# First batch of a Fourier-filter and feed-forward kernel: split PSUM evacuations, finer filter and x pieces, small operations on GpSimd, another order of the last units

## The chip, the cores and the metric

The kernel runs on one core of a Trainium2 chip. The metric is device time in microseconds (us) of one execution; the median over several executions counts. The core has four compute engines that the profile calls PE (TensorE, matrix products), DVE (VectorE), ACT (ScalarE) and POOL (GpSimd), and SP (SyncE), which here only issues DMAs. DMAs are issued on two queues: POOL's (software descriptors, q0 in the profile) and SP's (hardware descriptors, q1). Each engine takes its instructions in the order of the program; engines wait for each other by semaphores.

## The reference

Eight sequences of 3008 tokens by 256 channels are filtered in the frequency domain, and each token then goes through a gated feed-forward layer:

```python
X = rfft(x, axis=1)                        # x: 8 x 3008 x 256, float32
Y = X * (filt_r + 1j * filt_i)[None]       # 1505 frequencies x 256
t = irfft(Y, n=3008, axis=1).reshape(24064, 256)
h = t @ w_in                               # 256 x 2048
g = h * (1 / (1 + exp(-beta * h)))         # beta: 2048
out = g @ w_out                            # 2048 x 256, float32
```

## The kernel before

**Arithmetic.** The transform of length 3008 = 47 x 64 is done by matrix products in bfloat16, in four stages: stage 1 (table `t1`, 94 rows in, 96 out) mixes the 47-point index, stage 2 (`t2`, one 128 x 128 table for each of NK = 24 frequency groups) the 64-point index; the result is multiplied by the filter (`fr_sb`, `fi_sb`); stages 3 and 4 (`t3` with its rotated copy `t3s`, and `t4`) go back. The tables are computed on the chip at the start from index patterns (POOL iotas, DVE integer arithmetic, ACT sines). The feed-forward layer takes 512 tokens at a time: two matmuls give 128 hidden units (`hps`, L732), ACT applies the gate (L741), four matmuls accumulate the output (`acc`, L752).

**Two phases.** Batches 1 to 7 are filtered inside the feed-forward loop of the batch before, by a plan of steps (L655 to L718). Batch 0 has no such cover: it is filtered first, by an order written out by hand (L300 to L555), while only loads for later run beside it. The first `hps` matmul ends this first phase. The change touches the first phase alone.

**The first phase.** x of batch 0 is loaded as `x0` (32 columns of 94 rows) by five DMAs on POOL's queue (L182 to L192, 8, 8, 8, 4 and 4 columns). `s1_0(g)` (L247) is stage 1 on four columns for both halves of the channels (e = 0, 1) in a two-bank PSUM tile, and one evacuation to `aT`, on DVE or ACT; the last group is evacuated in halves by both. `spin` runs matmuls on zeros. `t2_half` writes half of `t2` (DVE arithmetic L226, L146; ACT sine L230), `t2_shift` derives the other half on DVE (L240, L242). `t3_part` transposes `t2` into `t3` on PE, `a0_turn` transposes `aT` into `a0`.

Then come six units (`units`, L469): three frequency thirds (kg) for e = 0, then three for e = 1. For each, `s2_0` (L422) has 8 matmuls and two DVE products with `fr_sb` and `fi_sb` (L434); `s3_0` (L437) has 16 matmuls and one evacuation to `zT` on ACT. After the three units of one e, `z_turn` transposes `zT` into `zz0`, and `f_0` or `s4_0` does stage 4 and evacuates to `y`. The last unit's evacuation is split over DVE and ACT, both reading one PSUM tile (`split`, L455), and the last two transposes of e = 1 share a tile in `z_pair` (L488). PSUM tiles come from `bank2` (three two-bank buffers) and `turn8` (two buffers of one bank).

**The filter.** Its values are needed on all 128 partitions. `load_filters` (L84) loads 32 partitions of `fr_sb` from SP and the 32 next to them, in reverse order, from POOL, and likewise for `fi_sb`; `spread(n)` (L462) copies a unit's `fr_sb` to the other 64 partitions and its `fi_sb` from there, with two POOL copies. Both DVE products of a unit wait for these copies. The pieces (`parts`, L93) are the three thirds of e = 0, then one third and two thirds of e = 1. SP holds its filter loads back until a two-element DMA, `seen` (L313), which reads the end of `t2` that `t2_shift` writes. Each queue has eight semaphores for DMAs, so a ninth DMA waits for the first to land.

**POOL's queue**, in the order of the program: x loads between iotas, six filter DMAs for parts 0 to 2, the halving of the first rows of `t4` (L298, after ACT has written `t4`), the two DMAs of part 3, `spread(0)`, two DMAs of part 4, `spread(1)`, `spread(2)`, the load of `w_in` (L502), two memsets, `spread(3)`, x of batch 1 (`load_x`), `spread(4)`, `load_x`, `spread(5)`, two `load_x`, and two scalings of `w_out` (L375).

Of the kernel before, what the change touches and what calls it, by code (L numbers as in the profile page):

```python
# [10 lines left out]
P = 128  # L11
# [11 lines left out]
M = 64  # L23
H = M // 2
NK = 24
# [11 lines left out]
def kernel(  # L37
# [52 lines left out]
            src = AP(filt.tensor, filt.offset + off * D + d0, [[N1 * D, H], [sg * D, n], [1, d1 - d0]])  # L90
            eng.dma_start(dst[q0 : q0 + H, k0:k1, d0:d1], src)

    parts = ((0, KH, 0, E2), (KH, 2 * KH, 0, E2), (2 * KH, NK, 0, E2), (0, KH, E2, D), (KH, NK, E2, D))  # L93

    t1 = consts.tile([NP, KP], BF16, name="t1", tag="t1")
    t4 = consts.tile([KP, NP], BF16, name="t4", tag="t4")
# [14 lines left out]
    def evac(dst, src, on_act, scale=None):  # L111
        if on_act:
            nc.scalar.activation(dst, src, ACT.Copy, scale=1.0 if scale is None else scale)  # L113
        elif scale is None:
            nc.vector.tensor_copy(dst, src)  # L115
        else:
            nc.vector.tensor_scalar_mul(dst, src, scale)  # L117
# [15 lines left out]
    def bank2(shape, dt=F32):  # L133
        return spsum.tile(shape, dt, name="sps", tag="sps")

    def turn8():
        return tpsum.tile([P, KH, P], BF16, name="tps", tag="tps")

    def small(name, dt=F32):
        return sp.tile([P, 1], dt, name=name, tag=name)  # L140
# [38 lines left out]
    def load_x0(j0, j1):  # L179
        load_rows(x0[:, j0:j1, :], 0, j0, j1)  # L180

    load_x0(0, 8)  # L182
    iota(ip[:], [[0, 1]], ch=1)
    iota(kc[:], [[1, NK], [0, 2]])
    iota(cc[:], [[0, NK], [1, 2]], base=1)
    load_x0(8, 16)
    iota(vi[:, :, :H], [[1, NK], [N1, H]])
    load_x0(16, 24)
    iota(vi[:, :, H:], [[1, NK], [-N1, H]], base=N1 * (M - 1))
    load_x0(24, 28)  # L190
    make_identity(nc, ident)
    load_x0(28, 32)  # L192
    for part in parts[:3]:
        load_filters(nc.gpsimd, *part)
    with nc.allow_non_contiguous_dma(reason="2048 values, once"):
        nc.sync.dma_start(beta_sb[:], moe_beta.rearrange("(fb fp) -> fp fb", fp=P))
    def shift_and(name, sh, mask):
        t = small(name, I32)
        if sh:
            nc.vector.tensor_scalar(t[:], ip[:], sh, mask, ALU.logical_shift_right, ALU.bitwise_and)  # L200
        else:
            nc.vector.tensor_scalar(t[:], ip[:], mask, None, ALU.bitwise_and)
        return t

    def affine(name, src, mul, add):
        t = small(name)
        nc.vector.tensor_scalar(t[:], src[:], mul, add, ALU.mult, ALU.add)
        return t

    n1s = affine("n1s", shift_and("n1_i", 1, M - 1), TURN / N1, 0.0)  # L210
# [34 lines left out]
    aTv = aT[:].rearrange("p e k (g m) -> p g e k m", m=MG)  # L245

    def s1_0(g, engines):  # L247
        ps = bank2([P, NDC, 512])
        for e in range(NDC):
            for i in range(MG):  # L250
                nc.tensor.matmul(
                    ps[:, e, i * KP : (i + 1) * KP],
                    lhsT=x0[:NP, g * MG + i, e * P : (e + 1) * P],
                    rhs=t1[:],
                    start=True,
                    stop=True,
                )
        src = ps[:, :, : MG * KP].rearrange("p e (m k) -> p e k m", k=KP)
        if len(engines) == 1:
            evac(aTv[:, g], src, engines[0])  # L260
        else:
            for e in range(NDC):
                evac(aTv[:, g, e], src[:, e], engines[e])

    def spin(n):
        ps = tpsum.tile([P, 512], F32, name="tps", tag="tps")
        for _ in range(n):
            nc.tensor.matmul(ps[:], lhsT=rest[:, :P], rhs=rest[:], start=True, stop=True)

    def a0_turn(kg, e, on_act):  # L270
        tp = turn8()
        for kk_ in range(KH):
            k4 = 4 * (kg * KH + kk_)
            nc.tensor.transpose(
                tp[:, kk_, :], aT[:, e, k4 : k4 + 4, :].rearrange("p c j -> p (c j)"), ident[:]
            )
        evac(a0[:, kg * KH : (kg + 1) * KH, e * P : (e + 1) * P], tp[:], on_act)
# [16 lines left out]
    def turn_t4():  # L294
        tp = turn8()
        nc.tensor.transpose(tp[:KP, 0, :NP], t1[:], ident[:NP, :NP])
        nc.scalar.activation(t4[:], tp[:KP, 0, :NP], ACT.Copy)
        nc.gpsimd.tensor_scalar(t4[0:4], t4[0:4], 0.5, None, ALU.mult)  # L298

    spin(17)  # L300
    t1v = t1[:].rearrange("p (k q) -> p k q", q=2)
    for q in range(2):
        nc.scalar.activation(t1v[:, :, q], sn[:NP], ACT.Copy, scale=q_p[q][:NP])
    t2_half(0)
    t2_half(1)
    s1_0(0, (False,))
    s1_0(1, (True,))
    spin(4)
    t2_shift(0)
    t2_shift(1)  # L310
    nc.vector.memset(t2[:, 0, M : P : M - 1], 0.0)
    seen = sp.tile([1, 2], BF16, name="seen", tag="seen")
    nc.sync.dma_start(seen[:], t2[:1, 1, P - 2 :])  # L313
    for part in parts:
        load_filters(nc.sync, *part)
    nc.scalar.activation(warm[:], ms[:], ACT.Silu)
    s1_0(2, (False,))
    s1_0(3, (True,))
    t3_part(0, True)
    v_i = shift_and("v_i", 5, 1)  # L320
    rot = (affine("rot0", v_i, 2.0, -1.0), affine("rot1", v_i, -2.0, 1.0))
    sgn = affine("sgn", c_i, -2.0, 1.0)
    c10 = sp.tile([P, P], BF16, name="c10", tag="c10")
    for c in range(2):
        nc.vector.tensor_copy(c10[:, c * M : (c + 1) * M], t2[:, 0, (1 - c) * M : (2 - c) * M])
    tiny = sp.tile([P, NFB], F32, name="tiny", tag="tiny")
    nc.vector.tensor_tensor(tiny[:], beta_sb[:], beta_sb[:], ALU.mult)
    nc.vector.tensor_scalar(tiny[:], tiny[:], 1e-12, 2e-6, ALU.is_lt, ALU.mult)
    nc.vector.tensor_tensor(beta_sb[:], tiny[:], beta_sb[:], ALU.add)
    nc.vector.reciprocal(rbeta_sb[:], beta_sb[:])  # L330
    s1_0(4, (False,))
    s1_0(5, (True,))
    t3_part(1, True)
    s1_0(6, (False,))
    turn_t4()
    s1_0(7, (False, True))
    t3_rotate(1, KH, False)
    a0_turn(0, 0, False)
    a0_turn(1, 0, True)
    t3_part(2, True)  # L340
    t3_rotate(KH, 2 * KH, False)

    r_sq.close()

# [45 lines left out]
    zz0 = zz0pool.tile([KP, J, D], BF16, name="zz0", tag="zz0")  # L390
    y_tile(0)

    def z_turn(e, hh, on_act):
        tp = turn8()
        for i in range(KH):
            j0 = (hh * KH + i) * KP
            nc.tensor.transpose(tp[:, i, :], zT[e][:, j0 : j0 + P], ident[:])  # L397
        evac(zz0[:, hh * KH : (hh + 1) * KH, e * P : (e + 1) * P], tp[:KP], on_act)
# [35 lines left out]
            nc.vector.tensor_tensor(r_t[:], ps[:], filt[:, ks, ds], ALU.mult)  # L434
            pq[n, c] = r_t

    def s3_0(n, split=False):  # L437
        kg, e = units[n]
        ps = bank2([P, KH, P])
        for c, tab in enumerate((t3, t3s)):  # L440
            src = pq.pop((n, c))
            for kk_ in range(KH):
                nc.tensor.matmul(  # L443
                    ps[:, kk_, :],
                    lhsT=src[:, kk_, :],
                    rhs=tab[:, kg * KH + kk_, :],
                    start=c == 0 and kk_ % 4 == 0,
                    stop=c == 1,
                    skip_group_check=True,
                )  # L450
        kq = P // J
        dst = zT[e][:, :WZ].rearrange("p (j k) -> p j k", k=KP)
        dst = dst[:, :, kg * KH * kq : (kg + 1) * KH * kq]
        src = ps[:].rearrange("p k (c j) -> p j (k c)", j=J)
        if split:  # L455
            for h in range(2):
                js = slice(h * J // 2, (h + 1) * J // 2)
                evac(dst[:, js], src[:, js], h == 1)
        else:
            evac(dst, src, True)  # L460

    def spread(n):  # L462
        kg, e = units[n]
# [21 lines left out]
            inv_scale,  # L485
        )

    def z_pair(e, hh, engines):  # L488
        tp = spsum.tile([P, 2, KH, P], BF16, name="sps", tag="sps")
        for h in range(2):  # L490
            for i in range(KH):
                j0 = ((hh + h) * KH + i) * KP
                nc.tensor.transpose(tp[:, h, i, :], zT[e][:, j0 : j0 + P], ident[:])
        for h in range(2):
            evac(zz0[:, (hh + h) * KH : (hh + h + 1) * KH, e * P : (e + 1) * P], tp[:KP, h], engines[h])

    load_filters(nc.gpsimd, *parts[3])
    spread(0)
    load_filters(nc.gpsimd, *parts[4])
    spread(1)  # L500
    spread(2)
    nc.gpsimd.dma_start(win_sb[:], moe_w_in.rearrange("(dc p) f -> p dc f", p=P))  # L502
    for e in range(NDC):
        nc.gpsimd.memset(zT[e][:, WZ:], 0.0)
    spread(3)
    load_x(1, 0)
    spread(4)
    load_x(1, 1)
    spread(5)
    load_x(1, 2)  # L510
    load_x(1, 3)
    load_wout(0)
    load_wout(WG)
    scale_wout(0)
    scale_wout(WG)

    s2_0(0)
    tp0 = turn8()
    nc.tensor.transpose(tp0[:, 0, :], c10[:], ident[:])
    nc.scalar.activation(t3s[:, 0, :], tp0[:, 0, :], ACT.Copy, scale=sgn[:])  # L520
    a0_turn(2, 0, True)
    s2_0(1)
    t3_rotate(2 * KH, NK, True)
    s3_0(0)
    s2_0(2)
    a0_turn(0, 1, True)
    s3_0(1)
    s2_0(3)
    a0_turn(1, 1, True)
    s3_0(2)  # L530
    s2_0(4)
    a0_turn(2, 1, True)
    z_turn(0, 0, True)
    z_turn(0, 1, True)
    s3_0(3)
# [2 lines left out]
    f_0(0, 1, True)  # L538
    z_turn(0, 2, True)
    z_turn(0, 3, True)  # L540
    f_0(0, 2, True)
    f_0(0, 3, True)
    s3_0(4)
    f_0(0, 4, True)
    f_0(0, 5, True)
    s3_0(5, True)
    f_0(0, 6, False)
    f_0(0, 7, True)
    z_turn(1, 0, False)
    z_turn(1, 1, True)  # L550
    z_pair(1, 2, (False, True))
    s4_0(1, 0, False)
    s4_0(1, 1, True)
    s4_0(1, 2, False)
# [246 lines left out]
```

## Time and profile before

| what | value |
| --- | --- |
| median of 5 runs | 787.03 us (785.72 to 788.42) |
| the profiled execution's own time | 785.72 us |
| its span | 783.9 us, so 1.8 us lie around the span |
| PE busy, share of the span | 762.8 us, 97% |
| DVE, ACT, POOL busy | 436.4, 561.7, 155.7 us |
| first matmul of the feed-forward loop | 42.95 us after the start of the span |

The page gives busy times, a picture of the span in 40 slices, the costliest groups of instructions and the chain of work that ended last. In a group, the columns are line, engine, operation, output and inputs with their shapes, count, then busy time and mean duration, then idle time before and who ended it. In a timeline, a line has the start, the duration, the engine, the line of the program and the tile, and in brackets the idle time before it. As most of the span is one steady loop bound by PE, the first 43 us have to be read by themselves.

### The profile page before, as it was taken

The page shows a single profiled execution, that of the slowest core. Times are in us where ns is not written, and L with a number is a line of the kernel's source. Part 1 is how long each engine was busy: PE and PEld are TensorE (multiplying, and loading weights), DVE is VectorE, ACT ScalarE, POOL GpSimd, SP SyncE. Part 2 cuts the span into 40 slices and gives each one's busy share as a digit, 9 for nine tenths or more (in the row PEclk, how much of TensorE's full clock was granted, in tenths as well). Part 3 has the DMA queues.
Part 4 walks back from the last instruction along what each step waited for, and adds up shares of the span by engine and source line. Part 5 has one row for each costly group of instructions (what it writes and reads, how often), then busy time and mean ns, then how long its engine had stood idle before and what let it go on. Part 6 is the DMA issues. An engine that isn't in the chain of part 4 may idle for free.

```text
span 783.9 us, 15141 instructions
## 1 busy us (share of the span) xinstructions
PE 762.8 (97%) x5971; PEld 544.1 (69%) x6063; DVE 436.4 (56%) x686; ACT 561.7 (72%) x827; POOL 155.7 (20%) x162
## 2 busy tenths in 40 slices
PE   7799999999999999999999999999999999999997
PEld 4666767766677667866678666786667766676665
DVE  8747754776557665566655675466655666321001
ACT  6887867766676766777667776677766777777776
POOL 7824300322012120122101222012200222000000
PEclk9999999999999999999999999999999999999999
DMA  9958276234831349133580416712164211500101
GB/s 184 229 164 199 93 211 167 68 88 110 234 89 57 96 120 243 51 78 105 116 241 28 123 60 158 198 57 86 49 188 118 65 48 49 155 28 28 55 28 54
DMA packets 87067, 88.50 MB, mean 113 GB/s; under 512 B 5629, under 2 KB 77821, under 8 KB 86997
## 3 DMA queue, kind: packets, MB, share of 16 engines
q1 hardware_dynamic: 82420, 72.37, 31.4%
q0 software_dynamic: 4576, 15.17, 11.2%
q8 instruction: 47, 0.77, 0.4%
q14 instruction: 24, 0.19, 0.1%
HBM read 54.47 MB, written 46.66 MB: 129 GB/s over the span
## 4 chain that ended last, share of the span: by engine, by line
PE 94%; DVE 2%; ACT 1%; issue 1%; DMA 1%; POOL 1%; SPq 0%; POOLq 0%; DVEq 0%; ACTq 0%
PE acc L752 43%; PE hps L732 39%; PE ps L578 3%; PE ps L645 3%; PE ps L623 3%; PE ps L594 2%; DMA fr_sb<-in_filt_r_dram 1%; ACT zz L113 0%; PE sps L443 0%; ACT zT L113 0%; PE tps L397 0%; DVE y L117 0%; DVE u L226 0%; POOL fr_sb L466 0%; DVE u L146 0%
## 5 line engine op out<-in xcount | busy, mean ns | idle before, releaser
L741 ACT ACTIVATE gT<-hps,beta_sb 128x512 bf16<-128x512 f32 x752 | 516.7, 687 | 207.6 <-PE hps L732 187.0
L752 PE MATMUL acc<-wout_sb,gT 128*128 128x256 bf16 x3008 | 453.4, 272 | 2.5
L732 PE MATMUL hps<-y,win_sb 128*128 128x512 bf16 (+7 forms) x1636 | 428.2, 350 | 1.0 <-DVE y L117 0.7
L752 PEld LDWEIGHTS <-gT 128*128 128x128 bf16 x3008 | 287.5, 98 | 126.2 <-issue 1.2
L613 POOL TENSOR_TENSOR yh<-a_t,b_t 128x512 bf16<-128x512 f32 x84 | 106.4, 1266 | 420.4 <-DVE b_t L612 419.5
L732 PEld LDWEIGHTS <-win_sb 128*128 128x128 bf16 x1728 | 164.8, 98 | 25.0 <-issue 1.0
L115 DVE COPY ost<-acc 128x512 f32<-128x512 f32 x93 | 59.9, 685 | 146.9 <-PE acc L752 146.9
L115 DVE CAST a<-ps 96x512 bf16<-96x512 f32 x104 | 70.9, 685 | 51.9 <-PE ps L578 47.9
L608 DVE TENSOR_TENSOR a_t<-ps,fr_sb 128x512 f32<-128x512 f32 x84 | 58.1, 691 | 71.1 <-PE ps L594 70.1
L117 DVE TENSOR_SCALAR y<-ps 128x376 bf16<-128x376 f32 x104 | 55.9, 547 | 59.3 <-PE ps L645 59.1
L609 DVE SCALAR_TENSOR_TENSOR b_t<-ps,fi_sb 64x512 f32<-64x512 f32 x84 | 58.2, 692 | 1.1
L612 DVE TENSOR_TENSOR b_t<-ps,fi_sb 64x512 f32<-64x512 f32 x84 | 57.4, 683 | 1.1
L115 DVE CAST z<-ps 128x512 bf16<-128x512 f32 x72 | 49.3, 684 | 1.7 <-PE ps L623 0.8
L645 PEld LDWEIGHTS <-zz 96*128 96x128 bf16 x448 | 29.8, 98 | 22.9
L578 PE MATMUL ps<-xg,t 94*96 94x512 bf16 x112 | 41.5, 381 | 0.6
L645 PE MATMUL ps<-t,zz 96*128 96x94 bf16 x448 | 34.7, 205 | 0.8
L623 PE MATMUL ps<-yh,t 128*128 128x256 bf16 x168 | 32.1, 273 | 0.6
L594 PE MATMUL ps<-a,t 128*128 128x256 bf16 x168 | 32.1, 273 | 0.3
L623 PEld LDWEIGHTS <-t 128*128 128x128 bf16 x168 | 16.3, 98 | 17.7
L594 PEld LDWEIGHTS <-t 128*128 128x128 bf16 x168 | 16.1, 98 | 15.2
L173 POOL DMA_DIRECT2D xg<-in_x_dram x24 | 12.4, 519 | 56.5 <-PE ps L578 56.5
L578 PEld LDWEIGHTS <-t 94*96 94x96 bf16 x112 | 13.8, 123 | 10.5
(104 smaller groups left out, 185.2 us busy)
## 6 DMA issues: line engine op xcount, KB each, us to landing
out_dram<-ost SPq DMA_DIRECT2D x46, 512.0 KB, 3.0
d<-a SPq DMA_DIRECT2D x28, 384.0 KB, 4.7
a<-d SPq DMA_DIRECT2D x28, 384.0 KB, 5.3
d<-z SPq DMA_DIRECT2D x28, 384.0 KB, 3.7
zz<-d SPq DMA_DIRECT2D x28, 384.0 KB, 6.7
xg<-in_x_dram POOLq DMA_DIRECT2D x24, 384.0 KB, 6.6
ws<-in_moe_w_out_dram SPq DMA_DIRECT2D x4, 512.0 KB, 12.1
xg<-in_x_dram POOLq DMA_DIRECT2D x4, 320.0 KB, 6.3
```

The lines of the kernel that those rows point to most:

```text
L115: nc.vector.tensor_copy(dst, src)
L578: nc.tensor.matmul(ps[:KP], lhsT=t1[:], rhs=xg[b, g][:NP, jj : jj + 2, :], start=True, stop=True)
L594: nc.tensor.matmul(ps[:, e, :], lhsT=t2[:, k0 + e, :], rhs=st["a2", b, g][:, kk + e, :], start=True, stop=True,)
L608: nc.vector.tensor_tensor(a_t[:], ps[:], fr_sb[:, ks, :], ALU.mult)
L609: nc.vector.scalar_tensor_tensor(b_t[:M], ps[M:], -1.0, fi_sb[M:, ks, :], ALU.mult, ALU.mult)
L612: nc.vector.tensor_tensor(b_t[M:], ps[:M], fi_sb[M:, ks, :], ALU.mult)
L613: nc.gpsimd.tensor_tensor(yh[:], a_t[:], b_t[:], ALU.add)
L623: nc.tensor.matmul(ps[:, e, :], lhsT=t3[:, 2 * i + e, :], rhs=yh[:, e, :], start=True, stop=True)
L645: nc.tensor.matmul(ps[:, e, :NP], lhsT=zz[:, j0 % JG + e, dc * P : (dc + 1) * P], rhs=t4[:], start=True, stop=True,)
L732: nc.tensor.matmul(hps[:, pos - t0 : pos - t0 + ln], lhsT=win_sb[:, dc, fb * P : (fb + 1) * P], rhs=ys[b][:, dc, n0 : n0 + ln], start=(dc ...
L741: nc.scalar.activation(gT[:], hps[:], ACT.Silu, scale=beta_sb[:, fb : fb + 1])
L752: nc.tensor.matmul(acc[tb // 2][:, tb % 2, :], lhsT=gT[:, tb * P : (tb + 1) * P], rhs=wout_sb[:, fb, :], start=(fb == 0 and tb % 2 == 0), ...
```

## The change

It has these parts, all in the first phase:

1. `parts`: the last piece (two thirds of e = 1) becomes two pieces, one for each unit; POOL issues part 4 after `spread(0)`, part 5 after `spread(1)`.
2. `x0` is loaded in pieces of 4, 8, 8, 8 and 4 columns.
3. `seen` reads an element that ACT's second sine writes, and not one that `t2_shift` writes; the SP loads stand behind it as before.
4. Stage 1: the first group is evacuated by ACT ahead of the sines, the others alternate; 13 and 3 spins in place of 17 and 4. The last group, the last unit's stage 3 and the last transposes get a PSUM tile for each evacuating engine (`z_pair` and `split` go).
5. Eight small operations (`rot`, `sgn`, `c10`, the guard on `beta_sb`) go from DVE to POOL, ahead of the DMAs of part 3. `t4` is made later, and its halving on POOL stands ahead of `spread(4)`.
6. `spread(3)` goes ahead of the load of `w_in`; the loads of x of batch 1 go behind `spread(4)` and `spread(5)`; the loads of `w_out` move in the text, not in SP's order.
7. Order: `t3_part` and `a0_turn` change places and engines, `t3_rotate(KH, 2 * KH)` goes from DVE to ACT, `a0_turn(2, 1)` ahead of `s3_0(2)`, `s3_0(4)` ahead of `f_0(0, 2)`, and `f_0(0, 4)` goes to DVE.

```diff
-    parts = (..., (0, KH, E2, D), (KH, NK, E2, D))
+    parts = (..., (0, KH, E2, D), (KH, 2 * KH, E2, D), (2 * KH, NK, E2, D))
...
-    load_x0(0, 8)          # then 8:16, 16:24, 24:28, 28:32
+    load_x0(0, 4)          # then 4:12, 12:20, 20:28, 28:32
...
     def s1_0(g, engines):
-        ps = bank2([P, NDC, 512])
+        one = len(engines) == 1
+        tiles = [bank2([P, NDC, 512])]
+        tiles.append(tiles[0] if one else bank2([P, NDC, 512]))
...
-    def a0_turn(kg, e, on_act):
-        tp = turn8()
+    def a0_turn(kg, e, on_act, wide=False):
+        tp = bank2([P, KH, P], BF16) if wide else turn8()
...
-    spin(17)
+    spin(13)
...
+    s1_0(0, (True,))
+    spin(3)
     t2_half(0)
     t2_half(1)
-    s1_0(0, (False,))
-    s1_0(1, (True,))
-    spin(4)
+    seen = sp.tile([1, 2], BF16, name="seen", tag="seen")
+    nc.sync.dma_start(seen[:], t2[:1, 1, M - 2 : M])
+    for part in parts:
+        load_filters(nc.sync, *part)
+    s1_0(1, (False,))
+    s1_0(2, (True,))
     t2_shift(0)
     t2_shift(1)
     nc.vector.memset(t2[:, 0, M : P : M - 1], 0.0)
-    nc.sync.dma_start(seen[:], t2[:1, 1, P - 2 :])
...
-    s1_0(2, (False,))
-    s1_0(3, (True,))
-    t3_part(0, True)
+    s1_0(3, (False,))
+    s1_0(4, (True,))
+    t3_part(0, False)
+    gp = nc.gpsimd
     v_i = shift_and("v_i", 5, 1)
-    rot = (affine("rot0", v_i, 2.0, -1.0), affine("rot1", v_i, -2.0, 1.0))
-    sgn = affine("sgn", c_i, -2.0, 1.0)
+    rot = (affine("rot0", v_i, 2.0, -1.0, gp), affine("rot1", v_i, -2.0, 1.0, gp))
+    sgn = affine("sgn", c_i, -2.0, 1.0, gp)
...
-        nc.vector.tensor_copy(c10[:, c * M : (c + 1) * M], t2[:, 0, (1 - c) * M : (2 - c) * M])
+        gp.tensor_copy(c10[:, c * M : (c + 1) * M], t2[:, 0, (1 - c) * M : (2 - c) * M])
...
-    nc.vector.tensor_tensor(tiny[:], beta_sb[:], beta_sb[:], ALU.mult)
-    nc.vector.tensor_scalar(tiny[:], tiny[:], 1e-12, 2e-6, ALU.is_lt, ALU.mult)
-    nc.vector.tensor_tensor(beta_sb[:], tiny[:], beta_sb[:], ALU.add)
+    gp.tensor_tensor(tiny[:], beta_sb[:], beta_sb[:], ALU.mult)
+    gp.tensor_scalar(tiny[:], tiny[:], 1e-12, 2e-6, ALU.is_lt, ALU.mult)
+    gp.tensor_tensor(beta_sb[:], tiny[:], beta_sb[:], ALU.add)
+    s1_0(5, (False,))
+    s1_0(6, (True,))
+    s1_0(7, (False, True))
+    t3_part(1, True)
+    t3_part(2, True)
+    t3_rotate(1, KH, False)
+    a0_turn(0, 0, False, True)
+    a0_turn(1, 0, False, True)
     nc.vector.reciprocal(rbeta_sb[:], beta_sb[:])
-    s1_0(4, (False,))
...
-    t3_rotate(KH, 2 * KH, False)
...
-    def s3_0(n, split=False):
+    def s3_0(n, engines=(True,)):
...
     load_filters(nc.gpsimd, *parts[3])
     spread(0)
     load_filters(nc.gpsimd, *parts[4])
     spread(1)
+    load_filters(nc.gpsimd, *parts[5])
     spread(2)
+    spread(3)
     nc.gpsimd.dma_start(win_sb[:], moe_w_in.rearrange("(dc p) f -> p dc f", p=P))
     for e in range(NDC):
         nc.gpsimd.memset(zT[e][:, WZ:], 0.0)
-    spread(3)
-    load_x(1, 0)
-    spread(4)
...
+    t3_rotate(KH, 2 * KH, True)
     s2_0(1)
+    a0_turn(2, 0, True)
     s3_0(0)
     s2_0(2)
+    t3_rotate(2 * KH, NK, True)
     a0_turn(0, 1, True)
+    turn_t4()
+    nc.gpsimd.tensor_scalar(t4[0:4], t4[0:4], 0.5, None, ALU.mult)
+    spread(4)
     load_x(1, 0)
-    spread(4)
     load_x(1, 1)
     spread(5)
     load_x(1, 2)
     load_x(1, 3)
...
     a0_turn(1, 1, True)
+    a0_turn(2, 1, True)
     s3_0(2)
     s2_0(4)
-    a0_turn(2, 1, True)
...
+    s3_0(4)
     f_0(0, 2, True)
     f_0(0, 3, True)
-    s3_0(4)
-    f_0(0, 4, True)
+    f_0(0, 4, False)
+    s3_0(5, (False, True))
     f_0(0, 5, True)
-    s3_0(5, True)
     f_0(0, 6, False)
     f_0(0, 7, True)
     z_turn(1, 0, False)
     z_turn(1, 1, True)
-    z_pair(1, 2, (False, True))
+    z_turn(1, 2, False, True)
+    z_turn(1, 3, True, True)
```

## The prediction

> **What bounds the kernel now.** I read the windows first, to see where PE is not full: only up to 43 us.
>
> ```profile
> 0.00:10.00 10.00, 7.72 (x53) 3.62 (x53) 7.65 (x23) 5.48 (x9) 8.77 (x21) 1.00 0.82 132
> 10.00:20.00 10.00, 6.70 (x107) 5.72 (x107) 8.52 (x23) 8.31 (x14) 5.95 (x10) 1.00 1.13 235
> 20.00:30.00 10.00, 7.98 (x126) 7.13 (x127) 6.97 (x6) 8.19 (x11) 8.37 (x11) 1.00 1.12 243
> 30.00:40.00 10.00, 7.35 (x125) 6.62 (x122) 6.70 (x8) 8.31 (x14) 8.23 (x9) 1.00 1.07 216
> 50.00:60.00 10.00, 9.95 (x68) 6.57 (x67) 1.57 (x3) 8.38 (x14) 4.77 (x4) 1.00 0.72 221
> ```
>
> Columns: length, busy us of PE, PEld, DVE, ACT, POOL, then granted clock, DMA share, GB/s. From 50 us PE is full, and nothing there is edited; so the kernel's time moves as the first `hps` matmul moves (42.95). Ahead of it no engine is full, the DMA engines are. So I took the waits up to 45 us, and then POOL's timeline, to find the order that sets the end.
>
> ```profile
> DVE pq_t L434 <- POOL fr_sb L466: 4.7, 5, 1.6
> POOL t L298 <- ACT t L297: 2.4, 1, 2.4
> POOL fr_sb L466 <- DMA fr_sb<-in_filt_r_dram: 2.0, 2, 1.3
> ACT zz L113 <- DVE zz L115: 0.6, 1, 0.6
> ACT zT L113 <- DVE zT L115: 0.2, 1, 0.2
> ```
>
> ```profile
> 2.06 0.15 POOL L143 IOTA ip<- 128x1 int32 x1
> 2.14 0.27 POOL L143 IOTA kc<- 128x48 int32 x1
> ...
> 14.15 0.48 POOL L298 TENSOR_SCALAR t<-t 4x94 bf16<-4x94 bf16 x1 [2.41 <-ACT t L297]
> 14.59 0.66 POOL L91 DMA_DIRECT2D fi_sb<-in_filt_i_dram x1
> ...
> 16.52 1.03 POOL L466 COPY fr_sb<-fr_sb 64x1024 f32<-64x1024 f32 x1 [0.69 <-DMA fr_sb<-in_filt_r_dram]
> ...
> 18.59 0.67 POOL L91 DMA_DIRECT2D fi_sb<-in_filt_i_dram x1
> ...
> 19.94 1.03 POOL L466 COPY fr_sb<-fr_sb 64x1024 f32<-64x1024 f32 x1
> ...
> 22.13 1.03 POOL L466 COPY fr_sb<-fr_sb 64x1024 f32<-64x1024 f32 x1
> ...
> 29.19 1.03 POOL L466 COPY fr_sb<-fr_sb 64x1024 f32<-64x1024 f32 x1 [1.34 <-DMA fr_sb<-in_filt_r_dram]
> ```
>
> The DVE products wait for POOL's copies, and between 16.52 and 27.8 POOL itself never waits: POOL's queue is the pace of the units. `spread(0)` starts when SP's first filter piece lands (issued 10.58, 5.77 later). From unit 2's products (DVE, 23.28 to 25.62) the chain goes on by ACT: 25.62 to 42.95 is 17.33 us.
>
> **The change part by part.** I call S0 the start of `spread(0)`, 16.52 before.
>
> *When POOL gets to its small operations.* They wait for `v_i` on DVE. x pieces of 8 columns land at 6.6, 9.0 and 10.9 (1.26 + 5.3, 2.54 + 6.5, 3.89 + 7.0), about 0.25 us a column. So 4, 12 and 20 columns land near 5.7, 7.8 and 9.9 (estimates). 17 spins ended at 6.4, the last ones 0.22 apart, so 13 end near 5.5 and don't hold stage 1. DVE: evacuation of group 1 from 8.4 (0.95), `t2_shift` and memset (8.51 to 10.23 before, 1.7), group 3 (0.95), `t3_part(0)` (0.69, the row of the `a0` copy), `v_i` (0.14): 12.8, less 0.2 of overlap, 12.6. Before, POOL stood at `t4` until 14.15. The landing of x late by 0.5 would move this by 0.5.
>
> *Eight small operations on POOL* (1 to 64 elements per partition; three of them each wait for the one before). On DVE they take 0.95 us (11.25 to 12.20). On POOL nothing like them is shown. From below: Iota 128x1, 0.15 each, 1.2 in all. From above: TENSOR_SCALAR 4x94, 0.48 each, 3.8. I take the 48-element iota, 0.26, which is nearest in size: 2.1. A gain is excluded, as POOL did none of them before. The page GPSIMD Engine Reference of the Trainium skill (section 4.1) speaks against this part: elementwise work belongs on VectorE, roughly twice as fast. By its factor the eight would cost 1.9, an estimate.
>
> *Part 3's two DMAs* take 1.35 (18.59 to 19.94). So POOL's queue reaches `spread(0)` at 12.65 + 2.1 + 1.35 = 16.1; bounds 15.2 and 17.8.
>
> *The landing that it waits for.* ACT now evacuates group 0 (0.79) ahead of the sines, about 6.3 to 7.1, so the second sine ends near 8.7 (8.49 before). `seen` goes out then and not at 9.80, SP's first filter piece near 9.6 and not at 10.58. It lands at 15.4 if all of that second counts, at 16.4 if none does.
>
> ```profile
> q0 software_dynamic: 524, 1.96, 103.0%
> q1 hardware_dynamic: 88, 0.08, 3.1%
> ```
>
> This is the DMA view of 28.5 to 38 us, a stretch in which a `w_out` load on SP's queue (q1) was waiting all along: POOL's queue (q0) took nearly everything. x and POOL's filter pieces are still moving at 9.6 to 13, so part of the second is lost. I take S0 = 16.2. The page DMA: Bandwidth & Descriptors (Queues, rings and completion order) says that an engine goes round between the rows packet by packet; with POOL's larger packets nothing would be gained, and S0 would be 16.4, 0.2 us more.
>
> *POOL up to unit 2.* Two copies take 2.07 (16.52 to 18.59), two DMA issues 1.35. Part 5 is now issued ahead of `spread(2)`, so that this starts at S0 + 2 x (2.07 + 1.35) = S0 + 6.84 = 23.04, not at 22.13. Unit 2's products follow one copy later (1.09) and take 2.34: they end at 26.47, 0.85 us later than 25.62. Here is the main cost: the 1.35 us of part 5 moved ahead of unit 2, against some 0.3 won at S0. From both sides: S0 of 15.4 gives 0.0, 17.8 gives +2.4.
>
> *POOL after that.* `spread(3)` at S0 + 9.0 = 25.2 (25.23 before). Then `w_in` and memsets (1.03) and the halving of `t4` (0.45): `spread(4)` at S0 + 12.6 = 28.8; the 1.34 of waiting for a landing goes, as the piece is half as large and issued no later than 18.6. Two x loads (1.1): `spread(5)` at S0 + 15.8 = 32.0 (31.83 before). The DVE products of units 4 and 5 are then within 0.2 us of before and do not decide. If ACT had not written `t4` by 28.3 (its place in ACT's order gives about 24), the halving would hold `spread(4)`, both x loads and `spread(5)`.
>
> *The way to the end on ACT.* ACT loses `a0_turn(2, 1)` (0.92 from start to next start) and `f_0(0, 4)` (0.39), and its two waits on DVE for a shared tile (0.8 together): at most 2.1 us. But the first of these filled the time in which PE transposes `zT` (0.65), which now shows as idle. `f_0(0, 4)` needs one of two `turn8` buffers, free only after ACT's evacuation of `f_0(0, 2)`; `s3_0(5)` is queued on PE behind it. And the two waits of ACT lie beside DVE's evacuations, which end the chain (DVE `y`, 41.96, then `hps`). Bounds 0 and -2.1; I take -0.3, near the first, since DVE's rows on that stretch stay as they are.
>
> *Covered.* `w_in`, issued near 27.3, landed 12.0 after issue: 39.3, needed at 43. x of batch 1, issued up to 34.7 and landing 8.6 (11.2 at worst) later, is read from 44 to 50. POOL scales `w_out` by about 39, needed at 45.6. Should one be late, its lateness adds in full. `t3_rotate(KH, 2 * KH)` costs ACT 1.3 near 17, where it waits for POOL anyway; `reciprocal` waits for POOL's guard on `beta_sb`, and the products behind it wait for `spread(0)`, later on the same queue. Spins, stage 1's split tiles and `t3_part`'s change of engine end by 16.0, before S0.
>
> Sum: +0.85 - 0.3 = +0.55. Against the profiled execution 785.72 + 0.55 = 786.3; this is the fastest of the five, the median stands 1.31 above it, so 787.6.
>
> **The rivals.**
> *Small operations at the upper row (slower).* At 0.48 each S0 is 17.8, and the sum +2.4 - 0.3 = +2.1: 789.1. It decides from 0.41 each, where the sum passes 1.57. For it: the 4x94 row is the only tensor operation of that size on POOL. Against: it has 94 elements, most of the eight 16 or fewer. Chance 0.3, with other delays on POOL's queue.
> *The tail gives most of its 2.1 (faster).* With S0 at 15.4 and -1.9 the sum is -1.9: 785.1. For it: ACT is busy 8.3 of 10 us in 30 to 40. Against: DVE and PE take turns with it in the chain. Chance 0.08.
> *The earlier filter loads do nothing.* S0 is 16.4, the sum +0.75, 787.8: hardly another result. It lies in the likeliest case, which has 0.62.
>
> **How the numbers follow.** Some 0.2% (1.57 us) is what a measurement of this kernel can tell from no change. The likeliest case is +0.55 with S0 of 15.4 to 17.2 and a tail of 0 to -1. The range goes from S0 of 15.4 with a tail of -1 (786.0) to S0 of 17.8 with none (789.5). Faster 0.08, within 0.62, slower 0.30.
>
> **What would show it.** In POOL's timeline after: small operations from 12.6, `spread(0)` near 16.2, two DMA issues ahead of `spread(2)` and this near 23.0, no wait of POOL before `spread(4)`; unit 2's products ending near 26.5; first `hps` near 43.5. Wrong would be: small operations outside 1.2 to 3.8 in all, a wait for `t4` or `w_in`, a tail shorter by more than 1, a granted clock below 1.00 (PE has an idle stretch of over 1 us before 10, with fewer spins), or any change after 45 us.

## The result, and the profile after

| | before | after |
| --- | --- | --- |
| median | 787.19 us (48 runs, 785.31 to 790.28) | 789.18 us (27 runs, 787.68 to 791.41) |
| profiled execution, and its span | 785.72, 783.95 | 789.41, 787.08 |
| first `hps` matmul | 42.95 | 45.73 |
| from there to the end of the span | 741.00 | 741.35 |
| time outside the span | 1.77 | 2.33 |

The changed kernel takes 1.0025 times as long (95% interval 1.0017 to 1.0034): slower by 2.0 us. The profiled executions lie 3.69 us apart, because that of before was one of its fastest: the median span of 34 executions of before, run beside the first experiments, is 785.9, that of 28 executions of after 786.9. The 3.69 us are 2.78 ahead of the first `hps`, 0.35 between it and the end of the span, and 0.56 outside the span. Only the first part is where the prediction looked.

The windows of after, with the columns of the prediction (length, busy us of PE, PEld, DVE, ACT, POOL, granted clock, DMA share, GB/s):

```profile
0.00:10.00 10.00, 6.98 (x39) 3.07 (x40) 5.45 (x19) 4.57 (x8) 8.66 (x21) 1.00 0.82 118
10.00:20.00 10.00, 7.84 (x94) 7.36 (x91) 7.04 (x15) 6.23 (x8) 4.84 (x14) 0.66 1.13 238
20.00:30.00 10.00, 7.71 (x118) 6.56 (x115) 8.67 (x10) 9.04 (x13) 9.68 (x12) 1.00 1.02 222
30.00:40.00 10.00, 6.90 (x116) 6.37 (x117) 6.76 (x7) 8.03 (x12) 9.63 (x14) 1.00 0.97 177
```

Two things are new: 14 GB/s less in the first 10 us, and a clock of 0.66 in the second. POOL's timeline shows the copies late (the line numbers of after are a few higher than before):

```profile
14.36 0.34 POOL L208 TENSOR_SCALAR rot<-v_i 128x1 f32<-128x1 int32 x2 [2.21 <-DVE v_i L201]
...
15.83 0.22 POOL L333 TENSOR_TENSOR beta_sb<-tiny,beta_sb 128x16 f32<-128x16 f32 x1
16.05 0.64 POOL L91 DMA_DIRECT2D fi_sb<-in_filt_i_dram  x1
...
18.71 1.03 POOL L469 COPY fr_sb<-fr_sb 64x1024 f32<-64x1024 f32 x1 [1.44 <-DMA fr_sb<-in_filt_r_dram]
...
24.05 0.58 POOL L91 DMA_DIRECT2D fi_sb<-in_filt_i_dram  x1
...
25.25 1.04 POOL L469 COPY fr_sb<-fr_sb 64x1024 f32<-64x1024 f32 x1
```

The small operations take 1.69 us in all (14.36 to 16.05), POOL's queue reaches `spread(0)` at 17.27, and then it stands 1.44 us for SP's first filter piece. This was issued 0.55 us earlier than before (10.03 against 10.58) and landed 2.20 us later (18.55 against 16.35). On DVE, the first product does not start right behind that copy either:

```profile
18.73 0.69 DVE L115 COPY a<-sps 128x1024 bf16<-128x1024 bf16 x1 [2.53 <-PE sps L277]
19.58 0.69 DVE L115 COPY a<-sps 128x1024 bf16<-128x1024 bf16 x1 [0.16 <-PE sps L277]
...
20.35 1.16 DVE L435 TENSOR_TENSOR pq_t<-sps,fr_sb 128x1024 bf16<-128x1024 f32 x1
```

The evacuations of `a`, which wait 2.53 us for PE's transposes, stand ahead of it in DVE's queue. So the first product starts 1.64 us after `spread(0)`; before it was 1.06 (16.52 to 17.58). The 2.78 us are then: `spread(0)` later by 2.19, the first product behind it by 0.58, and together 0.01 for the rest (unit 0's second product ends at 22.64 and the first `hps` follows 23.09 later; before 19.94 and 23.01).

This split follows one row of events. It does not say what each cause would give back if it alone were taken away, because two paths are late by almost the same amount. The chain of work that ended last does not pass `spread(0)` in this profile. It goes from the second x piece through PE's matmuls, from 12.88 on at half clock, to DVE's evacuation of `a` (start, duration, what):

```profile
2.52 6.79 DMA x<-in_x_dram
...
16.13 1.71 PE tps L285 x16
17.84 1.72 PE sps L277 x16
...
19.58 0.70 DVE a L115
...
21.43 1.22 DVE pq_t L435
```

So with the filter piece landing as early as before, unit 0's first product would still have stood behind that evacuation, which ends at 20.27. The other path goes over POOL's copies to unit 2's products (end 28.68). By the 0.72 us between these and unit 2's `zT` before, it would have started this `zT` at 29.40 (an estimate); ACT's own order starts it at 29.47.

### The profile page after: what moved, and what is told of

Same layout as the page of the kernel before. It is cut to its first block, busy times and chain, and to the rows that moved or that the text cites. A ratio compares the mean times of both kernels' runs of the same rounds, so it can differ in the third digit from the quotient of the medians.

```text
span 787.1 us, 15139 instructions
## 1 busy us (share of the span) xinstructions
PE 765.0 (97%) x5966; PEld 546.7 (69%) x6058; DVE 436.0 (55%) x678; ACT 560.9 (71%) x827; POOL 158.1 (20%) x172
## 4 chain that ended last, share of the span: by engine, by line
PE 95%; ACT 3%; DMA 1%; issue 1%; DVE 0%; POOL 0%; POOLq 0%; ACTq 0%
PE acc L751 43%; PE hps L731 39%; PE ps L577 3%; PE ps L644 3%; PE ps L622 3%; PE ps L593 2%; DMA x<-in_x_dram 1%; ACT zz L113 1%; ACT zT L113 1%; ACT a L113 0%; PE sps L254 0%; PE tps L285 0%; ACT y L113 0%; PE tps L398 0%; PE sps L277 0%
```

## The experiments

All were timed beside the kernel before, in three groups of four, each on another chip: a_again, a_spin, a_x8 and a_dve (median of the kernel before 787.69 us), b_xg, a_xg, a_xg_p5 and b_xg_x4 (787.70), and the last four (787.54). So a time is compared with others of its group, or by its ratio to the kernel before. Marks from each run's one profile, in us:

| run | last x piece landed | SP's first filter piece issued, landed | `spread(0)` | unit 0's products end | first `hps` | clock at half |
| --- | --- | --- | --- | --- | --- | --- |
| before | 13.10 | 10.58, 16.35 | 16.52 | 19.94 | 42.95 | none |
| after | 14.28 | 10.03, 18.55 | 18.71 | 22.64 | 45.73 | 12.88 to 19.71 |
| a_again | 14.06 | 10.26, 17.54 | 17.70 | 22.32 | 45.40 | 13.34 to 20.16 |
| a_spin | 14.03 | 10.19, 17.76 | 17.91 | 21.34 | 45.05 | none |
| a_x8 | 12.59 | 10.58, 16.10 | 16.25 | 21.01 | 44.10 | 14.01 to 17.42 |
| a_dve | 13.70 | 10.06, 17.07 | 17.24 | 22.38 | 45.52 | 12.93 to 19.75 |
| b_xg | 12.81 | 10.60, 15.95 | 16.11 | 20.43 | 43.48 | none |
| b_xg_x4 | 13.74 | 11.23, 17.91 | 18.07 | 21.49 | 44.50 | 44.63 to 48.04 |
| a_xg | 14.05 | 9.31, 17.12 | 17.27 | 20.80 | 44.34 | 11.26 to 14.67 |
| a_xg_p5 | 13.66 | 9.29, 17.38 | 17.54 | 21.91 | 45.00 | 11.35 to 18.17 |
| b_xg_spin | 12.76 | 10.66, 16.04 | 16.20 | 20.73 | 43.99 | 16.18 to 19.59, 33.24 to 36.66 |
| b_xg_spin_tail | 13.64 | 10.42, 16.71 | 16.88 | 20.30 | 43.66 | none |
| a_xg_p5_spin | 13.76 | 9.57, 17.89 | 18.04 | 21.46 | 45.00 | 22.17 to 25.58 |
| a_xg_p5_spin_x8 | 12.40 | 10.10, 15.47 | 16.81 | 20.23 | 43.51 | none |

(Names with a_ are made from the changed kernel, with b_ from the kernel before. The clock column leaves out the start and the end of the kernel.)

### Once more, the changed kernel as it is (a_again)

> The changed kernel unaltered, profiled once more, as the base for its variants on the same chip. Its first profile had three things that the one of before had not: x pieces of 28 and 32 columns landing at 13.2 and 14.3 us (before 11.8 and 13.1), SP's first filter piece landing 8.5 us after its issue (before 5.8), and the TensorE clock at half from 12.9 to 19.7. Theory L (the landing is a property of the new pieces and order): again about 18.5 for SP's first piece, spread(0) near 18.7, first hps near 45.7. Rival C (chance of one execution): landing near 16.4, spread(0) near 17.4, where POOL's own queue ends, first hps near 44.5. Whether the clock halves again is open to both.

789.9 us, ratio 1.0025 (1.0012 to 1.0037). The filter piece lands at 17.54, a microsecond earlier than in the first profile, and the first `hps` still comes at 45.40: the late start is no accident of one execution, but the landing alone does not set it. From unit 0's products to the first `hps` it is 23.08 us here and 23.09 after. This profile has a further loss that the first one does not have, in the steady loop:

```profile
PE ps L593 <- DMA a<-d: 1.1, 1, 1.1
```

It is taken up below.

### The x pieces (a_x8, b_xg_x4)

Undone in the changed kernel, and done alone in the kernel before (with a copy that is explained below):

```diff
-    load_x0(0, 4)      ...  load_x0(4, 12)  ...  load_x0(12, 20)  ...  load_x0(20, 28)
+    load_x0(0, 8)      ...  load_x0(8, 16)  ...  load_x0(16, 24)  ...  load_x0(24, 28)
```

> The changed kernel with x in pieces of 8, 8, 8, 4 and 4 columns as before. Theory X (the smaller first piece delays the rest of x and with it all filter pieces behind): x of 28 columns at 11.8, SP's first filter piece at 16.5 to 17, spread(0) near 17, first hps near 44.2, 1.5 us less than the unaltered one. Theory S (seen is earlier, and SP's packets hold up POOL's) or C: x pieces as in the unaltered one's order, no gain, within 0.3 us.

> The kernel before with that copy, and with only the x pieces of the change (4, 8, 8, 8, 4 columns instead of 8, 8, 8, 4, 4). X: the small first piece makes the later pieces land 0.3 to 2 us later (profile after: 9.32, 11.18, 13.15, 14.28 against 8.99, 10.88, 11.84, 13.10 and then the filter pieces behind them), so SP's first filter piece lands at 17.5 or later instead of 16.35, spread(0) starts at 17.7 or later, and the first hps comes 1.0 to 2.2 us later than in the kernel before with the copy; median about 787.3. N: what counts is when the first batch's work ends, not when the pieces land; first hps within 0.4 us, median within 0.4 us of it.

a_x8: 789.12 us (1.0015, 1.0005 to 1.0024); `spread(0)` at 16.25, first `hps` at 44.10, as X said, but the median gains 0.8 us on a_again and not 1.5, and the intervals of the two overlap. b_xg_x4: 788.21 us against 786.87 of b_xg, and `spread(0)` at 18.07 against 16.11, first `hps` 1.02 us later. X holds in both directions. Over all fourteen profiles SP's first filter piece lands at 17.07 to 18.55 with the pieces of the change, at 15.47 to 16.71 with those of before, whenever it is issued (9.29 to 11.23). The windows from 4 to 6 us show where it begins, first before, then after:

```profile
4.00:5.00 1.00, 1.00 (x6) 0.47 (x5) 0.90 (x9) 0.58 (x3) 1.00 (x2) 1.00 1.00 188
5.00:6.00 1.00, 1.00 (x7) 0.41 (x5) 0.97 (x2) 0.24 (x2) 1.00 (x3) 1.00 1.09 197
```

```profile
4.00:5.00 1.00, 1.00 (x3) 0.30 (x2) 0.90 (x9) 0.61 (x3) 1.00 (x2) 1.00 1.19 139
5.00:6.00 1.00, 1.00 (x4) 0.41 (x3) 0.96 (x2) 0.21 (x1) 1.00 (x3) 1.00 0.95 160
```

The last column is GB/s: 49 and 37 less. In b_xg_x4 it is 154 and 131, in a_x8 197 and 205. (In a_xg_p5_spin the shortfall comes later, from 6 to 8 us: 160 and 139, against 217 and 209 in a_xg_p5_spin_x8.) In all fourteen profiles the bytes moved up to 12 us go with the pieces: 1.45 to 1.69 MB in the eight with those of the change, 1.72 to 1.83 in the six with those of before. What is not moved by then is moved later: the last x piece, and the filter pieces behind it. Why the smaller first piece has this effect is not shown. POOL issues one x piece each 1.3 us in both kernels, so there may be less in the queue; but the DMA share, in the column before, is no lower in sum (1.19 and 0.95 against 1.00 and 1.09), so the packets took longer for their bytes.

### The small operations back on DVE (a_dve)

```diff
-    gp = nc.gpsimd
+    gp = nc.vector
```

> The changed kernel with the eight small operations on DVE. They took 1.69 us on POOL (14.36 to 16.05), but spread(0) then stood 1.44 us waiting for a filter piece. Theory L: spread(0) starts when the piece lands, so no more than 0.3 us is won, and DVE's 1 us delays the evacuations of stage 1: within 0.5 us of the unaltered one. Rival P (POOL's queue sets spread(0)): 1.7 us less, first hps near 44.0.

789.92 us, as a_again (789.9). POOL now waits 2.67 us for the filter piece instead of 0.98: the small operations lay beside this wait. Theory L holds, P falls, and with it the prediction's rival of the upper row.

### Matmuls to hold the clock (a_spin)

```diff
     s1_0(0, (True,))
-    spin(3)
+    spin(10)
...
     s1_0(2, (True,))
+    spin(4)
...
     s1_0(4, (True,))
+    spin(4)
```

> The changed kernel with 10 spins in place of 3 after the first group, and 4 more after the groups 2 and 4 of stage 1: the clock should be granted in full, and nothing else is altered. Theory L: the half clock delayed unit 0's products by at most 0.6 us (20.35 against 19.8, where the first copy of spread(0) ends) and units 1 and 2 not at all, as their copies on POOL come later: first hps within 0.3 us of the unaltered one's, time within 0.3 us. Rival K (the clock makes the loss): first hps 2 us earlier, about 43.7, time 2 us less.

788.74 us (1.0014, 1.0004 to 1.0024), 1.2 us below a_again, between the two theories; the intervals overlap. Its profile keeps the full clock, and unit 0's first product starts 1.07 us after `spread(0)` (17.91, 18.98). So the half clock is the 0.58 us above: it slows the transposes that DVE's evacuations of `a` wait for. The first `hps` gains only 0.35 us on a_again. `spread(0)` itself is 0.21 us later in a_spin, and the next path is close: `zT` of unit 2 waits for its products.

The stretches at half clock last 3.41 or 6.83 us in every profile. Windows of this length show what precedes them (after):

```profile
9.47:12.88 3.41, 1.83 (x37) 1.57 (x37) 2.85 (x7) 2.60 (x4) 1.27 (x3) 1.00 1.06 234
12.88:16.30 3.42, 2.84 (x35) 2.70 (x33) 3.17 (x7) 1.34 (x3) 1.77 (x9) 0.50 1.12 239
16.30:19.71 3.41, 3.41 (x34) 3.32 (x32) 0.82 (x2) 2.30 (x3) 1.98 (x3) 0.50 1.19 236
19.71:23.12 3.41, 2.62 (x41) 2.15 (x39) 3.01 (x5) 2.50 (x4) 3.25 (x6) 1.00 1.15 232
```

In the first of these PE waits for x 1.01 us ahead of 11.23 and for ACT 0.57 ahead of 12.65; it is busy for 1.83 of 3.41 us (54%), and the next windows have the clock at 0.50, until one is full (3.41). The longest wait for x, 1.80 us ahead of 9.36, lies in the window before (6.06 to 9.47), which was busy for 47% and still kept the clock.

### A load that overtakes another (b_xg, a_xg)

In a_again, PE stands 1.14 us at 66.45 for `a<-d`, the first read-back of the second batch's stage 1. POOL's next x load (`xg`) and SP's `a<-d` are issued at almost the same time. The lead of `xg`, and the time that `a<-d` then took to land: after 0.05, 5.48; before 0.10, 6.08; a_spin 0.17, 5.85; a_x8 0.26, 7.02; a_dve 0.39, 7.31; a_again 0.48, 7.47. The last three have a wait of PE there (0.6, 1.1, 1.1), the first three none. POOL's moment is set by its last `w_out` scaling, SP's by a store; both shift with the first batch. The experiment holds `xg` back by a copy of two elements that reads what `a<-d` loads:

```diff
+    held = consts.tile([1, 2], BF16, name="held", tag="held")
+    def hold(b):
+        nc.gpsimd.tensor_copy(held[:], st["a2", b, 0][:1, 0, :2])
...
+                at(o + 14, hold, 1)
                 for g in range(4):
                     at(o + 14 + 3 * g, load_x, 2, g)
```

> The kernel before, with one tiny copy on POOL that reads the first column tile of the second batch (a<-d) put ahead of the third batch's first x load, so that POOL issues this load after a<-d has landed instead of at about the same time (56.50 against 56.60 before). Two theories of the stretch after the first hps. G: the two loads race; where POOL's is 0.25 us or more ahead, a<-d takes 7.0 to 7.5 us instead of 5.5 to 6.1 and PE stands 0.6 to 1.1 us before L593 (or its like) at about 65 us, and this is most of the spread of both kernels; then this run has no such wait, first hps 42.9 (within 0.4), rest after it 741.0, median 785.8 (785.3 to 786.4), runs within 1 us of each other, against a median of about 787.5 for the kernel before. H: the spread comes from elsewhere; the median stays within 0.5 us of the kernel before and the spread stays 3 us or more.

> The changed kernel with the same copy ahead of the same load. G: first hps 45.4 (45.0 to 45.8), no wait of PE for a<-d, median 788.2 (787.7 to 788.8), spread under 1.5 us, so the change costs 2.4 us against the run of the kernel before with the same copy, all of it ahead of the first hps. H: median 789.5 or more, spread as in the changed kernel (3.5 us).

POOL's timeline of b_xg:

```profile
60.53 0.17 POOL L658 COPY held<-a 1x2 bf16<-1x2 bf16 x1 [3.35 <-DMA a<-d]
61.02 1.05 POOL L173 DMA_DIRECT2D xg<-in_x_dram  x2 [0.32 <-PE hps L738]
```

`a<-d` now lands 3.25 us after its issue (57.22 to 60.47; 3.22 to 3.46 in the eight profiles with the copy), and PE waits for it in none of them. So the mechanism is shown, but G's size is not: b_xg has 786.87 us (ratio 0.9991, 0.9979 to 1.0004), between G and H, and its spread is still 3.3 us; a_xg has 788.59 (1.0015, 1.0007 to 1.0023), where G had it, with a spread of 2.3. What is left in b_xg goes with the mean granted clock of an execution: 785.8 to 786.3 at 0.999 and 1.000, 786.8 to 787.6 at 0.997, 787.1 to 789.1 at 0.995 and 0.994. That stretches of half clock cause this is read from that row only; where in the executions without a profile they fell is not known.

### Where part 5 is issued (a_xg_p5)

```diff
-    load_filters(nc.gpsimd, *parts[5])
     spread(2)
+    load_filters(nc.gpsimd, *parts[5])
```

> The changed kernel with that copy, and part 5's two loads issued after spread(2) instead of ahead of it, where the prediction had +0.85 us from this place. P: the products of unit 2 set the path, so the 1.2 us that spread(2) comes earlier move the first hps from 45.4 to 44.3 and the median by 1.0 us. A: in the profile after, ACT's evacuations of a (27.65 to 29.41) end just when the products of unit 2 are done, and zT of unit 2 starts at 29.47 behind them, so the earlier product meets ACT's own order; spread(2) comes 1.2 us earlier all the same, but the first hps gains 0.3 us at most and the median 0.3 or less.

788.72 us against 788.59 of a_xg: nothing. `spread(2)` starts 5.45 us after `spread(0)`, as before (5.61) and not as in a_xg (6.68), and unit 2's products end at 26.49 instead of 27.38. But ACT goes on only at 28.75:

```profile
22.62 1.02 ACT L113 ACTIVATE zT<-sps 128x1024 bf16<-128x1024 f32 x1 [0.51 <-PE sps L446]
23.55 1.32 ACT L293 ACTIVATE t3s<-t,rot 128x512 bf16<-128x512 bf16 x2
24.77 1.01 ACT L113 ACTIVATE a<-tps 128x1024 bf16<-128x1024 bf16 x1
...
25.80 1.02 ACT L113 ACTIVATE zT<-sps 128x1024 bf16<-128x1024 f32 x1
26.92 1.94 ACT L113 ACTIVATE a<-tps 128x1024 bf16<-128x1024 bf16 x2
28.75 1.03 ACT L113 ACTIVATE zT<-sps 128x1024 bf16<-128x1024 f32 x1
```

From the first `zT` to the third ACT hardly waits: 6.13 us of its own work, in which the rotation of `t3s` for the last third (before, it ran ahead of the first `zT`, at 19.36) and one of the two evacuations at 26.92 (of `a0_turn(2, 1)`, before behind unit 2's `zT`) are new. Theory A holds, for a profile at half clock up to 18.17. In a_xg, whose clock was back at 14.67, the first `hps` comes 23.54 us after unit 0's products and unit 2's path is the later one by about 0.45, so at full clock part 5 could still cost that much. In the five runs where nothing later holds ACT (after, a_again, a_x8, a_dve, a_xg_p5) it is 23.08 to 23.14 us from the end of unit 0's products to the first `hps`, while from unit 2's products it varies from 17.05 to 18.51.

### All three undone (a_xg_p5_spin, a_xg_p5_spin_x8)

The edits of a_xg_p5 and a_spin together, and then those of a_x8 as well.

> The changed kernel with the copy of b_xg, part 5 after spread(2), and the idle matmuls of a_spin. Theory of two paths: from the end of unit 0's second product to the first hps there are 23.09 us of ACT's own order (after 23.09, a_again 23.08, a_x8 23.09, a_dve 23.14, a_xg_p5 23.09), and from the end of unit 2's products 17.1; whichever is later decides. At full clock (a_spin) the second decided (27.90, 17.15), so here part 5's place counts: products of unit 2 end 1.1 us earlier against spread(0), first hps 23.1 after unit 0's products, 44.2 to 44.6 where the filter pieces land at 17.8 as in a_spin, median 787.2 to 788.0. If part 5 never counts: from unit 0's products to the first hps again 23.5 or more, median 788.3.

> The same with the x pieces of the kernel before (8, 8, 8, 4, 4). If late landing, half clock and part 5 are all there is to the loss, spread(0) starts at 16.2, unit 0's products end at 19.9 to 20.1, first hps 43.0 to 43.3, and the median is that of the kernel before with the copy (785.9 to 786.6). If there is a further cause (the small operations on POOL, the split evacuations), unit 0's products end at 20.7 or later, first hps 43.8 or later, median 787.2 or more.

a_xg_p5_spin: 788.26 us (1.0007, 0.9997 to 1.0018), first `hps` at 45.00, 23.54 after unit 0's products: expected were 23.1 and at most 788.0. Its profile fell to half clock from 22.17 to 25.58, where unit 1's matmuls took 0.98 to 1.03 us instead of 0.62; from unit 1's `zT` on it is ACT's own 19.19 us, as in after (19.20). So this run does not tell what part 5 costs at full clock. Part 5 and the copy together gained 0.5 us on a_spin by the medians (0.3 when each is taken against the kernel before of its group), which is less than the intervals of the two can tell apart.

a_xg_p5_spin_x8: 787.11 us (0.9994, 0.9985 to 1.0003), first `hps` at 43.51. This lies between the two theories. POOL's own queue now sets `spread(0)` (16.81, 1.34 after the landing). The small operations take 1.81 us there and start at 13.73, against 12.88 in a_x8, because `v_i` is later on DVE; that the extra matmuls push it is likely, but was not tried. The first phase is within 0.6 us of before. Which of the parts that no run undid by itself costs the rest (the earlier `seen`, the finer filter pieces, the order of stage 1 and its evacuations) is open. What is left after the first phase shows best against the next run.

### The kernel before, improved (b_xg_spin, b_xg_spin_tail)

b_xg with `spin(4)` made `spin(7)` and a `spin(4)` after `s1_0(3)`, seven idle matmuls more; then the same with the last part of the change, and two idle matmuls into `hps` ahead of the first step:

```diff
-    spin(4)
+    spin(7)
...
     s1_0(3, (True,))
+    spin(4)
```

> The kernel before with the copy of b_xg and six more idle matmuls on PE's waits for the first batch's x (three more after group 1, four behind group 3 less what was there). K: what is left of the spread in b_xg (785.8 at a granted clock of 1.0, 786.9 at 0.997, 788.5 and more at 0.994) are stretches of half clock in the first 20 us, which more matmuls there prevent; then most runs have a clock of 0.999 or more and the median is 785.9 to 786.3. T: the half clock falls at the joint to the steady loop (44.6 in b_xg_x4), which these matmuls don't touch; median 786.7 to 787.1, clocks as in b_xg.

> The same, with of the change only its last part (order of the last units, wide turns, the last evacuation from two tiles, f_0(0,4) on DVE), and two idle matmuls ahead of the first hps. The prediction's term of -0.3 us for the tail: from the end of unit 2's products to the first hps 17.0 instead of 17.33, first hps 42.6 where the filter pieces land as before; if the two matmuls also hold the clock at the joint, the median is 785.4 to 785.9, the fastest version of all; if the tail gives all of its 2.1 us, 784.

b_xg_spin: 786.12 us, ratio 0.9986 (0.9975 to 0.9996): faster than both kernels. Its median is where K had it, but neither theory holds: 4 of its 12 executions have a clock of 0.999 or more, as in b_xg, and its profile falls twice, at 16.18 and 33.24, not at the joint. Which part of the gain is the matmuls' is open, since its interval overlaps that of b_xg.

b_xg_spin_tail: 786.49 us (0.9989, 0.9979 to 0.9999), not the fastest. From unit 2's `zT` to the first idle matmul it is 16.53 us, against 16.61 to the first `hps` in the kernel before: the tail gains 0.08 there (0.35 in the changed kernel, 16.26, which also has `a0_turn(2, 1)` ahead of that `zT`). The idle matmuls did not fill the wait; they stood behind it, like `hps`, and cost 0.43.

### The end of the kernel

a_xg_p5_spin_x8 is 0.99 us slower than b_xg_spin by the medians, and this is not the first phase as far as the profiles show it: the first `hps` comes at 43.51 against 43.99 (where b_xg_spin's profile has two stretches at half clock). In the trace, SP's last instructions wait for the DMA semaphores one after another, 0.06 us each. Before, the two last stores are on the last two of the list; SP is through 0.06 us after the second has landed. In the changed kernel, with two more filter loads on SP's queue, the stores fall on the second and the third, and six more waits follow: 0.37 us. All nine profiles of kernels with the change's loads show this, the five others don't.

Outside the span the same two kernels differ by 0.48 (medians of 12 executions: 2.26 and 1.78). The DMA view of the last microseconds (queue, kind: packets, MB, share of the engines' time), before and after:

```profile
q1 hardware_dynamic: 544, 0.52, 15.4%
```

```profile
q1 hardware_dynamic: 544, 0.52, 15.4%
q14 instruction: 1, 0.01, 0.3%
```

After has one more packet, of the kind instruction (8192 bytes), 2.08 us behind the last instruction. Eight of the nine profiles with the change's loads have it, with 2.23 to 2.40 us outside the span; the ninth (a_xg_p5_spin) has none, and 1.89. The other five have none and 1.77 to 1.92. That a load of code at the end costs these 0.3 us or more fits all fourteen; it was not tried by itself. The 0.37 in the span and the 0.48 outside it make 0.85 of the 0.99 us.

## Why the prediction was right or wrong

The time lies in the range, but the likeliest case (787.6, within 0.2%) was not the one: it came out 1.6 us slower, in the case that had a chance of 0.30, and not by that case's mechanism. That this case had 789.1, next to the measured 789.18, is luck: it rested on small operations of 0.48 us each, which took 1.69 us in all, not 3.8.

- **S0 was the step that failed**: 16.2, bounds 15.4 to 17.8; measured 18.71, and 17.24 to 18.07 in the seven other profiles with the change's pieces. The prediction let the landing of SP's first filter piece lie between "all of the earlier issue counts" and "none does". It counted the same bytes in the queue ahead, but not that fewer of them are moved by then: with the small first x piece 49 and 37 GB/s are missing at 4 to 6 us in the profile after, and the filter piece lands 1.4 (a_again against a_x8) to 2.0 us (b_xg_x4 against b_xg) later. With the pieces of before S0 is 16.25. Besides, the prediction had only POOL's path from S0 on. In the profile after, the path over PE's transposes to DVE's evacuations of `a` is as late, so S0 alone is not the whole of it. With 18.71 in place of 16.2 the prediction's sum would be +3.1 us; the first `hps` came 2.78 later.
- **When POOL gets to its small operations**: 12.6 against 14.36 (12.88 in a_x8), mostly for the same reason; 12 and 20 columns landed at 9.32 and 11.18, not at 7.8 and 9.9. The estimate of 0.25 us a column came from pieces of eight.
- **Eight small operations**: 2.1 against 1.69, inside 1.2 to 3.8. On DVE they took 0.95, a factor of 1.8 for the stretch. The Trainium skill's GPSIMD Engine Reference (section 4.1) gives its factor of about two for operations with two inputs only and calls those with one input roughly line-rate, and six of the eight have one. So the prediction's 1.9 came near by luck: the two rows with two inputs took 0.20 and 0.22 us against 0.17 and 0.18 on DVE, those with one 1.3 to 1.7 times as long as on DVE. And a_dve shows that they cost nothing here, since POOL waits for the landing anyway.
- **Part 5**: spread(2) came 6.54 after S0 (6.84 foreseen) and unit 2's products ended 3.06 us later than before, as the mechanism has it. But the step from there to the end was wrong: moving the loads back gained nothing (a_xg_p5, in a profile partly at half clock). "From unit 2's products the chain goes on by ACT" held before; in the changed kernel ACT's order from unit 0's `zT` on is as late. The prediction placed the rotation that ACT takes over from DVE beside a wait of ACT, but not the other one, which gives way to it and stands in that chain (24.27 to 25.50 in after).
- **The tail**: -0.3 against -0.35 from unit 2's `zT` on: right in size. b_xg_spin_tail, with the last units alone, gains only 0.08 of it there, so most goes with `a0_turn(2, 1)`, which the change puts ahead of that `zT`, into ACT's order before it. That ACT's two waits for a shared tile were worth next to nothing agrees: DVE's `y` ends the chain before (41.96) and after (44.74).
- **The clock**: the prediction named the fall as a way to be wrong (an idle stretch of PE over 1 us, with fewer spins), and gave it no price. It came, after a window with waits of 1.01 and 0.57 us (the wait of 1.80 lay in the window before, which kept the clock), and is worth 0.6 us between `spread(0)` and the first product in the profile after.
- **"Nothing after 45 us"**: wrong by 0.91 us in the profiled executions. 0.35 of it lie in the span, where SP's waits at its end account for 0.37, and 0.56 outside the span. Besides, the read-back at 65 us loses up to 1.1 us in three of the changed kernel's profiles (a_again, a_x8, a_dve).
- **The rival that earlier filter loads do nothing** was the nearest in kind: issued 0.55 us earlier, the piece gained nothing. The prediction's page DMA: Bandwidth & Descriptors (Queues, rings and completion order) has the engines go round between the queue rows packet by packet, from which the prediction took that an earlier issue behind POOL's larger packets is worth nothing. No run shows the round itself, but the landings agree: with the change's pieces an issue at 9.29 landed at 17.38, one at 10.06 at 17.07 and one at 11.23 at 17.91.

## What to carry to other kernels

A smaller first piece made the first data land earlier here (5.08 instead of 6.60), and what came behind it later, with pieces issued at a fixed pace: look at GB/s in the first microseconds, not only at the DMA share, before a queue is called full. When one path is moved, list the paths that end within a microsecond of it; here filter landing, PE's transposes and ACT's order all met at unit 0, and undoing any one of them gained 1.2 us at most by the medians (a_spin). And take the end of the kernel into the sum: a change of the number of DMAs moved 0.37 us there.

## What was not expected of the hardware

- The clock of PE fell without a window in which PE was idle throughout. Of the windows of 3.41 us up to 50 us in fourteen profiles, the ten before a fall had PE busy for 33 to 55%, with no idle stretch over 2.02 us; with 57% or more it never fell, and between 47 and 55% it went either way (six stayed). The Trainium skill's page TensorE: Matmul & The Clock Gate (section Why this matters for your kernels) asks for no idle gap over about 3 us between bursts; here gaps of 0.70 and 0.90 us in one window were enough (b_xg_x4, 53% busy), so the measurement decides. The length of the window, 3413 ns on that page, agrees with the stretches here.
- `a<-d` lands 3.2 to 3.5 us after its issue when POOL's load waits for it, 5.5 to 6.1 with POOL's load issued up to 0.17 us before it, and 7.0 to 7.5 with a lead of 0.26 us or more (three profiles each).
